# A one-core decode kernel: both MLP weights go to the head of the load queue, and the MLP is computed ahead of the query projection

## The chip, the core and the metric

The kernel runs on one core of a Trainium2 chip. The metric is the device time of one execution in microseconds (us). A difference of 0.2% is about the smallest that this measurement can tell from no change.

## The reference

One decode step for a batch of 4 tokens (`x` is 4 x 512). The input is normalised (`xn`), and two branches read it. Branch A is grouped-query attention: 32 query heads, 8 key/value heads, and of 4096 cached positions only the last W = 1024. Branch B normalises again, and runs a 512 to 1792 to 512 MLP. The output joins them.

```
xn = layernorm(x)
# branch A
q = xn @ wq                                  # 512 x 4096
k, v = last 1024 rows of the caches          # 8 kv heads, 128 wide, bf16
s = softmax(q k^T / sqrt(128)) v @ wo        # 4096 x 512
# branch B
h = gelu(layernorm(xn) @ w1 + b1)            # 512 x 1792
g = silu(h @ w2 + b2)                        # 1792 x 512
out = x + s * g
```

All data is bf16. What has to be loaded is 8 MiB of keys (8 heads x 1 MiB for the four batch entries), 8 MiB of values, 4 MiB of `wq`, 4 MiB of `wo`, and 1.75 MiB each of `w1` and `w2`: 27.5 MiB in all.

## The kernel before

**The order of work** is written out by hand. `add(engine, fn, deps)` appends one step to the program of one engine (`pe` TensorE, `dve` VectorE, `act` ScalarE, `gp` GpSimd), and `pg.dma("sp", ...)` appends a load to the program of SyncE (SP). Each engine runs its own list strictly in the order in which the steps were appended. A step first waits for its dependencies by semaphores, so a wait holds up everything behind it on that engine.

**The load queue** is SP's list: `load_k(0)`, `load_k(1)` (lines 206 to 217), `wq` in two halves of 2 MiB (219), `load_k(2)` to `load_k(7)`, then `load_v(0)`, `w1` (441), `load_v(1)`, `w2` (444), `load_v(2)` to `load_v(7)`, and `wo` in six pieces (449 to 455), the last of 128 KiB. The values of head g go into the buffer of the keys of head g, so `load_v(g)` waits for `t_last[g]`, the last transpose of that head's keys (212 to 214). The `wo` pieces wait for nothing but their place in the list.

**Front.** VectorE and ScalarE make both layernorms (247 to 264). TensorE meanwhile starts on the keys. A head's 32 key blocks are cut into 4 units of 8, so there are 32 units. `T(n)` (273) transposes the 8 blocks of unit n into PSUM and VectorE copies them out (285). There are three PSUM buffers `psK`, so `T(n)` waits for the copy of `T(n-3)`. `T(0)` to `T(7)` come first (339 to 341), then `f_xy` (343) transposes the two normalised inputs, giving `xT` for the query and `yT` for the MLP.

**Query.** `f_q` (357) multiplies `xT` with `wq`: 16 matmuls on the first half of `wq`, 16 on the second. The result is copied by VectorE and ScalarE (368, 369), transposed by `f_qT` (371), and copied into `qT` (379 to 382), which every score needs.

**Loop.** Lines 435 to 439 alternate `T(n)` and `S(n-8)`; `S` (288) computes the scores of one unit (8 matmuls with 16 columns), and after 4 units ScalarE takes the exponential of the head (306). The last 8 `S` follow without a `T` between them; the text calls these the S tail.

**Values.** `PV(g)` (310) does 32 matmuls with the values of head g, and one matmul with ones, `den` (322), that sums the denominators over the partitions. `epilogue(g)` (326) on VectorE reduces, inverts and scales (329, 332, 334). `PV(g)` waits for the exponential, for the load of V(g), and for `epilogue(g-2)`, whose PSUM it overwrites.

**MLP.** Four parts (386 to 433). `mlp1`: 14 groups of 4 matmuls with `w1` and one with the bias, then Square on ScalarE, two VectorE steps, Exp on ScalarE. `mlp2`: three VectorE steps that give `hT`. `mlp3`: 4 groups of 14 matmuls with `w2` and one with the bias, then Exp. `mlp4`: three VectorE steps that give `g`. TensorE does `mlp1` right behind `PV(0)`, and `mlp3` right behind `PV(1)` (495 to 505).

**Tail.** `to_rows` (457) regroups the attention output with 16 small matmuls, `wo` (478) does 128 matmuls in six batches, each waiting for its piece of `wo`, then come the product with `g` (512), a transpose (516), the residual (518) and the store (520).

Of the kernel before, what the change touches and what calls it, by code (L numbers as in the profile page):

```python
# [16 lines left out]
class _Program:  # L17
# [10 lines left out]
    def add(self, eng, fn, *deps):  # L28
        op = _Op(eng, fn, deps)
        self.ops[eng].append(op)  # L30
        return op
# [42 lines left out]
def bass_recurrent_scan__sliding_block_cached__mixer_channel_mlp__decode_kernel(  # L74
# [15 lines left out]
    AF = mybir.ActivationFunctionType  # L90
# [5 lines left out]
    HQ, HKV, DH = 32, 8, 128  # L96
# [4 lines left out]
    FC = F // 128  # L101
# [19 lines left out]
    wq_sb = sb([128, 4, HQ * DH], BF16)  # L121
    wo_sb = sb([128, HKV, 4, D], BF16)
    w1_sb = sb([128, 4, F], BF16)
    w2_sb = sb([128, FC, D], BF16)
# [21 lines left out]
    ident = sb([128, 128], BF16)  # L146
# [6 lines left out]
    xT = sb([128, 4, 32], BF16)  # L153
    yT = sb([128, 16], BF16)
    q_sb = sb([128, 2, 512], BF16)
    qT = sb([128, 128], BF16)
# [24 lines left out]
    psK = [nc.alloc_psum_tensor("psK%d" % i, [128, 1024], BF16) for i in range(NB)]  # L181
    psS = [nc.alloc_psum_tensor("psS%d" % i, [128, 512], F32) for i in range(2)]
    psO = [nc.alloc_psum_tensor("psO%d" % i, [128, 512], F32) for i in range(2)]
# [3 lines left out]
    pg = _Program(nc)  # L187
    add = pg.add
# [8 lines left out]
    def cache_rows(cache, g):  # L197

        return bass.AP(cache.tensor, g * SK * DH + WS * DH,
                       [[NC * DH, KR], [HKV * SK * DH, B], [1, NC * DH]])  # L200
# [5 lines left out]
    def load_k(g):  # L206
        d_k[g] = pg.dma("sp", "k%d" % g, lambda e: e.dma_start(  # L207
            kv_buf[:, g, :, :].rearrange("p c d -> p (c d)"), cache_rows(A_k_cache, g)),
            )

    def load_v(g):
        d_v[g] = pg.dma("sp", "v%d" % g, lambda e: e.dma_start(
            kv_buf[:, (HKV + g) % NS, :, :].rearrange("p c d -> p (c d)"), cache_rows(A_v_cache, g)),
            t_last[(HKV + g) % NS] if HKV + g >= NS else None)

    load_k(0)
    load_k(1)
    wq_r = A_wq.rearrange("(p c) n -> p c n", c=4)
    d_wq = [pg.dma("sp", "wq%d" % c, lambda e, c=c: e.dma_start(
        wq_sb[:, 2 * c:2 * c + 2, :], wq_r[:, 2 * c:2 * c + 2, :])) for c in range(2)]  # L220
# [52 lines left out]
    def T(n):  # L273
        g, u = n // NU, n % NU

        def fn(pe):
            last = None
            for j in range(UT):
                last = pe.transpose(psK[n % NB][:, j * 128:(j + 1) * 128],  # L279
                                    kv_buf[:, g, u * UT + j, :], ident[:, :])  # L280
            return last
        t = add("pe", fn, d_k[g], c_id, cp.get(n - NB), v_xyT if n >= LAG else None)
        if u == NU - 1:
            t_last[g] = t
        cp[n] = add("dve", lambda e: e.tensor_copy(kt_buf[:, n % NKT, :], psK[n % NB][:, 0:1024]),  # L285
                    t, sc.get(n - NKT))
# [52 lines left out]
    v_xyT = None  # L339
# [3 lines left out]
    def f_xy(pe):  # L343
# [8 lines left out]
    v_xT = add("dve", lambda e: e.tensor_copy(  # L352
        xT[:, :, 0:4], psK[1][:, 0:16].rearrange("p (c b) -> p c b", c=4)), t_xy, c_xT)
    v_xyT = add("dve", lambda e: e.tensor_copy(yT[:, :], psK[1][:, 16:32]), t_xy)


    def f_q(pe, half):
        last = None
        for c in (2 * half, 2 * half + 1):
            for m in range(HKV):  # L360
                s = m % 4
                last = pe.matmul(psO[m // 4][32 * s:32 * s + 32, 0:512], xT[:, c, :],  # L362
                                 wq_sb[:, c, m * 512:(m + 1) * 512],
                                 start=(c == 0), stop=(c == 3), tile_position=(0, 32 * s))
        return last
    add("pe", lambda pe: f_q(pe, 0), v_xT, d_wq[0])
    t_q = add("pe", lambda pe: f_q(pe, 1), d_wq[1])
    v_qr = [add("dve", lambda e: e.tensor_copy(q_sb[:, 0, :], psO[0][:, 0:512]), t_q),  # L368
            add("act", lambda e: e.activation(q_sb[:, 1, :], psO[1][:, 0:512], AF.Copy), t_q)]  # L369

    def f_qT(pe):
        last = None
        for k in range(8):
            last = pe.transpose(psK[1][:, k * 128:(k + 1) * 128],  # L374
                                q_sb[:, k // 4, (k % 4) * 128:(k % 4 + 1) * 128], ident[:, :])
        return last
    t_qT = add("pe", f_qT, v_xyT, *v_qr)

    for k in range(2):
        v_q = add("dve", lambda e, k=k: e.tensor_copy(  # L380
            bass.AP(qT, k * 64, [[128, 128], [16, 4], [4, 4], [1, 4]]),
            bass.AP(psK[1], k * 512, [[1024, 128], [32, 4], [1, 4], [128, 4]])), t_qT)

    mlp = {}

    def mlp1():
        def fn(pe):
            last = None
            for k in range(FC):
                o = psM[:, PS_H + k * 4:PS_H + (k + 1) * 4]  # L390
                for c in range(4):
                    pe.matmul(o, bass.AP(w1_sb, c * F + k, [[4 * F, 128], [FC, 128]]),  # L392
                              yT[:, c * 4:(c + 1) * 4], start=(c == 0), stop=False)
                last = pe.matmul(o, bass.AP(b1_sb, k, [[F, 1], [FC, 128]]), ones_bf[0:1, 0:4],  # L394
                                 start=False, stop=True)
            return last
        h = psM[:, PS_H:PS_H + FC * 4]
        t = add("pe", fn, v_xyT, d_w1, d_b1)
        a = add("act", lambda e: e.activation(u2_sb[:, :], h, AF.Square), t)  # L399
        v = add("dve", lambda e: e.tensor_scalar(t_sb[:, :], u2_sb[:, :], GELU_K, 1.0,  # L400
                                                 op0=ALU.mult, op1=ALU.add), a)
        v = add("dve", lambda e: e.tensor_tensor(t2_sb[:, :], t_sb[:, :], h, ALU.mult), v)
        mlp["e"] = add("act", lambda e: e.activation(ge_sb[:, :], t2_sb[:, :], AF.Exp,
                                                     scale=-GELU_A), v)

    def mlp2():
        h = psM[:, PS_H:PS_H + FC * 4]
        v = add("dve", lambda e: e.tensor_single_scalar(e1_sb[:, :], ge_sb[:, :], 1.0, ALU.add),
                mlp["e"])
        v = add("dve", lambda e: e.reciprocal(r_sb[:, :], e1_sb[:, :]), v)  # L410
        mlp["h"] = add("dve", lambda e: e.tensor_tensor(hT[:, :], h, r_sb[:, :], ALU.mult), v)  # L411

    def mlp3():
        def fn(pe):
            last = None
            for c in range(4):
                o = psM[:, PS_Z + c * 4:PS_Z + (c + 1) * 4]
                for k in range(FC):
                    pe.matmul(o, w2_sb[:, k, c * 128:(c + 1) * 128], hT[:, k * 4:(k + 1) * 4],  # L419
                              start=(k == 0), stop=False)  # L420
                last = pe.matmul(o, b2_sb[0:1, c * 128:(c + 1) * 128], ones_bf[0:1, 0:4],
                                 start=False, stop=True)
            return last
        t = add("pe", fn, mlp["h"], d_w2, d_b2)
        mlp["ez"] = add("act", lambda e: e.activation(
            ez_sb[:, :], psM[:, PS_Z:PS_Z + 16], AF.Exp, scale=-1.0), t)

    def mlp4():
        v = add("dve", lambda e: e.tensor_single_scalar(d1_sb[:, :], ez_sb[:, :], 1.0, ALU.add),
                mlp["ez"])  # L430
        v = add("dve", lambda e: e.reciprocal(rz_sb[:, :], d1_sb[:, :]), v)
        mlp["g"] = add("dve", lambda e: e.tensor_tensor(
            g_sb[:, :], psM[:, PS_Z:PS_Z + 16], rz_sb[:, :], ALU.mult), v)

    NUN = HKV * NU
    for n in range(LAG, NUN + LAG):
        if n < NUN:
            T(n)
        S(n - LAG)
    load_v(0)  # L440
    d_w1 = pg.dma("sp", "w1", lambda e: e.dma_start(
        w1_sb[:, :, :], B_w1.rearrange("(p c) f -> p c f", c=4)))
    load_v(1)
    d_w2 = pg.dma("sp", "w2", lambda e: e.dma_start(
        w2_sb[:, :, :], B_w2.rearrange("(p c) o -> p c o", c=FC)))
    for g in range(2, HKV):
        load_v(g)

    wo_r = A_wo.rearrange("(g p i) o -> p g i o", g=HKV, i=4)
# [44 lines left out]

    for g in range(HKV):
        PV(g)
        if g == 0:
            mlp1()
        if g >= 1:
            epilogue(g - 1)  # L500
        if g == 1:
            mlp2()
            mlp3()
        if g == 2:
            mlp4()
    epilogue(HKV - 1)
    rows = to_rows(0, HKV)
    for k in range(len(d_wo)):
# [65 lines left out]
```

## Time and profile before

| what | value |
|---|---|
| median of 4 runs | 77.29 us (77.23 to 77.46) |
| the profiled execution itself | 77.27 us |
| its span, first to last instruction | 75.4 us |
| around the span (77.27 less 75.4) | 1.9 us |
| mean granted TensorE clock | 0.744 of full speed |
| TensorE busy | 52.5 us (70%) |
| VectorE busy | 38.1 us (51%) |
| ScalarE, GpSimd busy | 9.0 and 4.5 us |
| loaded on SP's queue | 28.84 MB |
| mean rate over the span | 385 GB/s |

Every other time in this document that is taken from the profile is in microseconds from the start of this span. TensorE has two rows in the profile: PE is the matmuls, PEld the loads of their weights, which run beside them. The page also cuts the span into 40 slices of 1.9 us and gives the busy share of each in tenths. For a load, the trace gives the moment at which SP issued it and the time from there to its landing; an issue can be tens of microseconds ahead of the landing, since the queue holds many loads.

### The profile page before, as it was taken

Reading aid. Unit: us, or ns where it says so; the run is one execution under the profiler, and the core shown is the slowest. Engines: PE = TensorE matmul, PEld = TensorE weight load, DVE = VectorE, ACT = ScalarE, POOL = GpSimd, SP = SyncE. Lnnn points to the kernel's source line nnn. Section 1 sums busy time; section 2 is a strip of 40 time slices with the busy share of each in tenths; the row PEclk is TensorE's granted clock in tenths of the full one; section 3 lists DMA queues with packets and bytes.
Section 4 is the critical chain, followed back from the end, with each engine's and each line's share of the span. In section 5 each row is a group of like instructions: output and inputs, shape, how many; then the busy total and the mean of one; then the engine's idle time right before and its main releaser. Section 6 shows DMA issues by size and latency. Waiting matters only on the chain.

```text
span 75.4 us, 2396 instructions
## 1 busy us (share of the span) xinstructions
PE 52.5 (70%) x1095; PEld 46.5 (62%) x1107; DVE 38.1 (51%) x84; ACT 9.0 (12%) x16; POOL 4.5 (6%) x13
## 2 busy tenths in 40 slices
PE   0008993500558999999999972999729897845970
PEld 0008982200218999999999862999729865815950
DVE  0778997100033589999998400000592587782010
ACT  0611000000054030330330630000200000000000
POOL 6970000000000000000000000000000000000000
PEclk9999999985555599999999999555555555555555
DMA  0899999999999999999999998999999999999700
GB/s 2 276 405 404 449 444 443 426 435 378 417 452 417 417 422 439 430 400 473 404 417 456 403 458 379 426 417 426 435 417 439 404 413 417 417 406 421 274 20 2
DMA packets 4213, 28.99 MB, mean 385 GB/s; under 512 B 486, under 2 KB 619, under 8 KB 1644
## 3 DMA queue, kind: packets, MB, share of 16 engines
q1 hardware_dynamic: 4160, 28.84, 91.7%
q8 instruction: 8, 0.13, 0.6%
q10 hardware_dynamic: 44, 0.01, 0.1%
q14 instruction: 1, 0.01, 0.0%
HBM read 28.85 MB, written 0.00 MB: 383 GB/s over the span
## 4 chain that ended last, share of the span: by engine, by line
PE 57%; DMA 22%; DVE 10%; issue 5%; SPq 2%; ACT 0%
DMA wq_sb<-in_A_wq_dram 22%; PE psK L279 16%; PE psS L298 10%; PE psM L392 6%; PE psO L316 6%; PE psM L486 5%; DVE den_sb L329 4%; PE psM L394 3%; PE psO L362 3%; PE psM L419 3%; PE psS L322 2%; SPq L207 2%; DVE rden L332 1%; PE psK L374 1%; DVE OTb L334 1%
## 5 line engine op out<-in xcount | busy, mean ns | idle before, releaser
L279 PE MATMUL psK<-ident,kv_buf 128*128 128x128 bf16 x256 | 21.5, 239 | 5.9 <-DMA kv_buf<-in_A_k_cache_dram 5.9
L285 DVE COPY kt_buf<-psK 128x1024 bf16<-128x1024 bf16 x32 | 20.9, 689 | 2.7 <-PE psK L279 2.6
L279 PEld LDWEIGHTS psK<-ident,kv_buf 128*128 128x128 bf16 x256 | 17.3, 108 | 6.2 <-DMA kv_buf<-in_A_k_cache_dram 5.9
L298 PE MATMUL psS<-qT,kt_buf 128*128 128x16 bf16 x256 | 10.4, 170 | 0.6 <-issue 0.2
L298 PEld LDWEIGHTS psS<-qT,kt_buf 128*128 128x128 bf16 x256 | 9.6, 97 | 1.1 <-issue 0.3
L316 PEld LDWEIGHTS psO<-P_buf,kv_buf 128*128 128x128 bf16 x256 | 7.5, 103 | 2.1 <-issue 2.1
L316 PE MATMUL psO<-P_buf,kv_buf 128*128 128x16 bf16 x256 | 8.0, 174 | 1.0 <-DVE OTb L334 0.6
L392 PE MATMUL psM<-yT,w_sb 128*128 128x4 bf16 x56 | 5.7, 204 | 1.9 <-issue 1.8
L362 PE MATMUL psO<-wq_sb,xT 128*32 128x512 bf16 x32 | 2.9, 504 | 5.5 <-DMA wq_sb<-in_A_wq_dram 5.1
L306 ACT ACTIVATE P_buf<-psS 128x512 bf16<-128x512 f32 x8 | 4.8, 597 | 16.1 <-PE psS L298 16.1
L329 DVE TENSOR_REDUCE den_sb<-psS 128x16 f32<-128x512 f32 x8 | 5.5, 690 | 1.4 <-PE psO L316 1.2
L400 DVE TENSOR_SCALAR t_sb<-u_sb 128x56 f32<-128x56 f32 x1 | 0.2, 193 | 11.4 <-ACT u_sb L399 11.4
L392 PEld LDWEIGHTS psM<-yT,w_sb 128*128 128x128 bf16 x56 | 4.5, 153 | 2.3 <-issue 2.1
L362 PEld LDWEIGHTS psO<-wq_sb,xT 128*32 128x32 bf16 x32 | 0.8, 112 | 6.7 <-DMA wq_sb<-in_A_wq_dram 5.6
L368 DVE CAST q_sb<-psO 128x512 bf16<-128x512 f32 x1 | 0.7, 692 | 8.2 <-PE psO L362 8.2
L486 PE MATMUL psM<-OW,wo_sb 128*128 128x4 bf16 x128 | 3.7, 166 | 0.5 <-DVE OW L472 0.5
L486 PEld LDWEIGHTS psM<-OW,wo_sb 128*128 128x128 bf16 x128 | 3.6, 104 | 0.6 <-issue 0.6
L419 PE MATMUL psM<-hT,w_sb 128*128 128x4 bf16 x56 | 2.1, 167 | 1.8 <-DVE hT L411 1.8
L394 PE MATMUL psM<-ones_bf,b_sb 1*128 1x4 bf16 x14 | 3.0, 215 | 0.0
L419 PEld LDWEIGHTS psM<-hT,w_sb 128*128 128x128 bf16 x56 | 1.8, 105 | 1.9 <-DVE hT L411 1.9
L369 ACT ACTIVATE q_sb<-psO 128x512 bf16<-128x512 f32 x1 | 0.6, 597 | 14.7 <-PE psO L362 14.7
L332 DVE RECIPROCAL rden<-den_sb 128x16 f32<-128x16 f32 x8 | 2.0, 253 | 0.3
(63 smaller groups left out, 28.3 us busy)
## 6 DMA issues: line engine op xcount, KB each, us to landing
kv_buf<-in_A_k_cache_dram SPq DMA_DIRECT2D x8, 1024.0 KB, 21.4
kv_buf<-in_A_v_cache_dram SPq DMA_DIRECT2D x8, 1024.0 KB, 22.2
wq_sb<-in_A_wq_dram SPq DMA_DIRECT2D x2, 2048.0 KB, 14.0
w_sb<-in_B_w_dram SPq DMA_DIRECT2D x2, 1792.0 KB, 30.9
wo_sb<-in_A_wo_dram SPq DMA_DIRECT2D x3, 1024.0 KB, 24.6
wo_sb<-in_A_wo_dram SPq DMA_DIRECT2D x1, 512.0 KB, 21.4
wo_sb<-in_A_wo_dram SPq DMA_DIRECT2D x1, 384.0 KB, 18.1
wo_sb<-in_A_wo_dram SPq DMA_DIRECT2D x1, 128.0 KB, 17.9
```

What stands on the lines that cost most here:

```text
L279: last = pe.transpose(psK[n % NB][:, j * 128:(j + 1) * 128], kv_buf[:, g, u * UT + j, :], ident[:, :])
L285: cp[n] = add("dve", lambda e: e.tensor_copy(kt_buf[:, n % NKT, :], psK[n % NB][:, 0:1024]), t, sc.get(n - NKT))
L298: last = pe.matmul(psS[g % 2][:, c * 16:(c + 1) * 16], kt_buf[:, n % NKT, j * 128:(j + 1) * 128], qT[:, g * 16:(g + 1) * 16], start=False, ...
L306: ex[g] = add("act", lambda e: e.activation(P_buf[:, g, :], psS[g % 2][:, 0:512], AF.Exp, scale=SCALE), sc[n])
L316: last = pe.matmul(pso[:, 0:16], kv_buf[:, (HKV + g) % NS, c, :], P_buf[:, g, c * 16:(c + 1) * 16], start=(c == 0), stop=(c == NC - 1))
L329: v = add("dve", lambda e: e.tensor_reduce(den_sb[:, cs], bass.AP(psS[g % 2], 0, [[512, 128], [1, 16], [16, NC]]), AX.X, ALU.add), den[g])
L332: v = add("dve", lambda e: e.reciprocal(rden[:, cs], den_sb[:, cs]), v)
L362: last = pe.matmul(psO[m // 4][32 * s:32 * s + 32, 0:512], xT[:, c, :], wq_sb[:, c, m * 512:(m + 1) * 512], start=(c == 0), stop=(c == 3), ...
L392: pe.matmul(o, bass.AP(w1_sb, c * F + k, [[4 * F, 128], [FC, 128]]), yT[:, c * 4:(c + 1) * 4], start=(c == 0), stop=False)
L394: last = pe.matmul(o, bass.AP(b1_sb, k, [[F, 1], [FC, 128]]), ones_bf[0:1, 0:4], start=False, stop=True)
L419: pe.matmul(o, w2_sb[:, k, c * 128:(c + 1) * 128], hT[:, k * 4:(k + 1) * 4], start=(k == 0), stop=False)
L486: last = pe.matmul(psM[:, PS_W + c * 4:PS_W + (c + 1) * 4], wo_sb[:, g, i, c * 128:(c + 1) * 128], OW[:, i, g * 4:(g + 1) * 4], start=firs ...
```

## The change

On SP's list `w1` becomes the first load, ahead of the keys of head 0, and `w2` comes behind the keys of head 1, ahead of both halves of `wq`. The values are then loaded in one plain row. The four parts of the MLP are unchanged in themselves. Their calls move from between the `PV` steps to a place directly behind `f_xy`, ahead of `f_q`, on TensorE, VectorE and ScalarE alike.

```diff
+    d_w1 = pg.dma("sp", "w1", lambda e: e.dma_start(
+        w1_sb[:, :, :], B_w1.rearrange("(p c) f -> p c f", c=4)))
     load_k(0)
     load_k(1)
+    d_w2 = pg.dma("sp", "w2", lambda e: e.dma_start(
+        w2_sb[:, :, :], B_w2.rearrange("(p c) o -> p c o", c=FC)))
     wq_r = A_wq.rearrange("(p c) n -> p c n", c=4)
     d_wq = [pg.dma("sp", "wq%d" % c, lambda e, c=c: e.dma_start(
         wq_sb[:, 2 * c:2 * c + 2, :], wq_r[:, 2 * c:2 * c + 2, :])) for c in range(2)]
...
     v_xyT = add("dve", lambda e: e.tensor_copy(yT[:, :], psK[1][:, 16:32]), t_xy)
+    mlp = {}
...
+    mlp1()
+    mlp2()
+    mlp3()
+    mlp4()
...
-    load_v(0)
-    d_w1 = pg.dma("sp", "w1", lambda e: e.dma_start(
-        w1_sb[:, :, :], B_w1.rearrange("(p c) f -> p c f", c=4)))
-    load_v(1)
-    d_w2 = pg.dma("sp", "w2", lambda e: e.dma_start(
-        w2_sb[:, :, :], B_w2.rearrange("(p c) o -> p c o", c=FC)))
-    for g in range(2, HKV):
+    for g in range(HKV):
         load_v(g)
...
     for g in range(HKV):
         PV(g)
-        if g == 0:
-            mlp1()
         if g >= 1:
             epilogue(g - 1)
-        if g == 1:
-            mlp2()
-            mlp3()
-        if g == 2:
-            mlp4()
```

More of the change, by code (lines that the diff above doesn't have):

```diff
@@ L354, in bass_recurrent_scan__sliding_block_cached__mixer_channel_mlp__decode_kernel @@
     v_xyT = add("dve", lambda e: e.tensor_copy(yT[:, :], psK[1][:, 16:32]), t_xy)
[L357 to L382, printed above, removed]
     mlp = {}
@@ L433, in mlp4, with f_q, f_qT @@
             g_sb[:, :], psM[:, PS_Z:PS_Z + 16], rz_sb[:, :], ALU.mult), v)
+    mlp1()
+    mlp2()
+    mlp3()
+    mlp4()
+    def f_q(pe, half):
+        last = None
+        for c in (2 * half, 2 * half + 1):
+            for m in range(HKV):
+                s = m % 4
+                last = pe.matmul(psO[m // 4][32 * s:32 * s + 32, 0:512], xT[:, c, :],
+                                 wq_sb[:, c, m * 512:(m + 1) * 512],
+                                 start=(c == 0), stop=(c == 3), tile_position=(0, 32 * s))
+        return last
+    add("pe", lambda pe: f_q(pe, 0), v_xT, d_wq[0])
+    t_q = add("pe", lambda pe: f_q(pe, 1), d_wq[1])
+    v_qr = [add("dve", lambda e: e.tensor_copy(q_sb[:, 0, :], psO[0][:, 0:512]), t_q),
+            add("act", lambda e: e.activation(q_sb[:, 1, :], psO[1][:, 0:512], AF.Copy), t_q)]
+    def f_qT(pe):
+        last = None
+        for k in range(8):
+            last = pe.transpose(psK[1][:, k * 128:(k + 1) * 128],
+                                q_sb[:, k // 4, (k % 4) * 128:(k % 4 + 1) * 128], ident[:, :])
+        return last
+    t_qT = add("pe", f_qT, v_xyT, *v_qr)
+    for k in range(2):
+        v_q = add("dve", lambda e, k=k: e.tensor_copy(
+            bass.AP(qT, k * 64, [[128, 128], [16, 4], [4, 4], [1, 4]]),
+            bass.AP(psK[1], k * 512, [[1024, 128], [32, 4], [1, 4], [128, 4]])), t_qT)
     NUN = HKV * NU
```

## The prediction

> **What bounds the kernel now.** I read the 40 slices first, to see which resource is never idle.
>
> ```profile
> PE   0008993500558999999999972999729897845970
> PEclk9999999985555599999999999555555555555555
> DMA  0899999999999999999999998999999999999700
> ```
>
> The transfer engines are full from the second slice to the 37th, about 2 to 70 us. The change moves loads but adds and removes no byte, so the end of the stream should stay where it is. I then read when single loads land (issue plus time to landing).
>
> ```profile
> L219 SPq DMA_DIRECT2D wq_sb<-in_A_wq_dram x2: 563/590/616, 2.1 to 2.8; - x2
> ...
> DMA to landing us min/median/max: 11.2/14.0/16.8
> ```
> ```profile
> L454 SPq DMA_DIRECT2D wo_sb<-in_A_wo_dram x2: 435/2942/5449, 53.9 to 54.4; - x2
> ...
> DMA to landing us min/median/max: 17.9/18.0/18.1
> ```
>
> The halves of `wq` land at 2.1 + 11.2 = 13.3 and 2.8 + 16.8 = 19.6, the last piece of `wo` at 54.4 + 17.9 = 72.3. By the same view K0 lands at 5.9, K1 at 8.5, K2 at 22.0, K7 at 34.2, V7 at 62.3. From K2 to V7 lie 16.5 MiB and 40.3 us: 2.44 us per MiB. Last I read TensorE's timeline.
>
> ```profile
> 13.44 1.05 PE L362 MATMUL psO<-wq_sb,xT 128*32 128x512 bf16 x16 [0.32 <-DVE yT L354]
> 19.63 1.90 PE L362 MATMUL psO<-wq_sb,xT 128*32 128x512 bf16 x16 [5.14 <-DMA wq_sb<-in_A_wq_dram]
> ```
> ```profile
> 43.56 0.95 PE L316 MATMUL psO<-P_buf,kv_buf 128*128 128x16 bf16 x32
> ...
> 44.58 0.17 PE L392 MATMUL psM<-yT,w_sb 128*128 128x4 bf16 x1
> 46.57 0.26 PEld L392 LDWEIGHTS psM<-yT,w_sb 128*128 128x128 bf16 x3 [2.07 <-issue]
> 46.58 0.34 PE L392 MATMUL psM<-yT,w_sb 128*128 128x4 bf16 x3 [1.83 <-issue]
> ...
> 56.08 0.53 PE L419 MATMUL psM<-hT,w_sb 128*128 128x4 bf16 x14 [1.81 <-DVE hT L411]
> ...
> 68.91 3.71 PE L486 MATMUL psM<-OW,wo_sb 128*128 128x4 bf16 x128 [0.51 <-DVE OW L472]
> 72.66 0.18 DVE L512 TENSOR_TENSOR sg_sb<-psM,g_sb 128x16 f32<-128x16 f32 x1 [3.89 <-PE psM L486]
> ```
>
> TensorE waits for `wq` until 19.63 and from then on hardly at all. The 128 `wo` matmuls run without a hole from 68.91 to 72.63, 29 ns each. The last four need the piece that landed at 72.3, and come at 72.5. So two chains end together here: the stream at 72.3, and TensorE's work at 72.63. From the last matmul the span has 2.75 us left, which the change doesn't touch. **Whatever TensorE saves is worth nothing below a floor of about 72.6; whatever it loses counts in full.**
>
> **What the change takes from the late stage.** From PV(0) at 43.56 to the first `wo` matmul at 68.91 are 25.35 us. Without the MLP the stage is eight `PV` groups in a row. PV(4) starts at 61.25, so four groups with the regrouping behind them take 68.91 - 61.25 = 7.66 us. Two groups (62.53 to 65.36) take 2.83, or 1.415 each. Eight groups: 7.66 + 4 x 1.415 = 13.3 us. The MLP and its waits therefore cost 25.35 - 13.3 = **12.05 us**, 1.83 of it the hole at 44.75.
>
> **What it puts in front.** `w1` (1.75 MiB, 4.3 us) is now ahead of K0 and K1, and 3.5 MiB (8.6 us) ahead of the second half of `wq`. K0 lands at 5.9 + 4.3 = 10.2, K1 at 12.8, `w2` near 17, `wq` at 19.6 + 8.6 = 28.2. The cover for the MLP is thus mostly bought by the change itself. TensorE's steps in its new order:
>
> - T(0) to T(7): in the window from 5.9 to 10.3, 48 of these transposes take 4.4 us, 0.73 per unit. From 10.2 the eighth ends near 16.0, with K1 in time for T(4). Its copy (0.65) and `f_xy` with the copies behind it (0.78, from 12.66 to 13.44) give `yT` at 17.4. If the clock rises earlier, VectorE's 0.65 per unit from K1 on sets it: 16.4. I take 17.25.
> - `mlp1`: 14 groups at 0.482 (46.58 to 53.33 holds them) make 6.75. A group takes as long at clock 1.0 (ahead of 47) as at 0.5. Ends at 24.0.
> - Square, Exp and `mlp2`: Square 0.24, Exp 0.25, three VectorE steps with gaps 0.98 (55.06 to 56.04). ScalarE still holds the square-root table; the load for Exp, 1.28 at 22.20 in the row of line 306, now falls between Square and Exp and hides only 0.45 of VectorE work. Chain 2.75, against 2.0 with the load hidden. TensorE stands idle: its next step in line is `mlp3`. 26.75.
> - `mlp3`: 2.4 (56.08 to 58.47). 29.15. `w2` is long there. `mlp4` is off TensorE's path.
> - `f_q`: all 32 matmuls now come behind the wait; before, 16 of them hid in it. At clock 0.5 sixteen took 1.93 (19.63 to 21.56), at 1.0 1.05. The MLP's narrow matmuls ran from 47 on at 0.5, busy as PE was, so I take 3.86, with 2.1 as the lower end. **Ends at 33.0, against 21.56: 11.45 us later.** `wq`, at 28.2, is not what is waited for.
>
> From `f_q` to PV(0) I leave the 22.0 us of before (21.56 to 43.56): K2 to K7 land from 30.6 to 42.8, ahead of their use. The clock came up at 26.4 there, 4.9 us behind `f_q`. A unit takes 1.05 us at 0.5 and 0.65 at 1.0, and a step of the clock lasted 3.4 us or multiples, so this is worth up to 0.6 less or 1.2 more. The bounds of the delay are 8.1 (16.4, a hidden table load, `f_q` at full clock) and 12.65.
>
> **The hole at 44.75** names no releaser. Both MLP weights had landed (40.9, 47.7 for the one used later). But one of eight transfers of another kind starts at 44.2:
>
> ```profile
> q8 instruction: 8, 0.13, 0.6%
> ```
>
> Between the starts of the fetches from 32.0 to 70.5 the PE and PEld rows count 1530 instructions in six stretches, 255 each. The hole follows the fastest stretch, S tail and PV(0), some 65 instructions per us, and I read it as a fetch that came late. The change takes 70 + 60 matmuls with as many weight loads, 260 instructions, from behind this place to ahead of it: all but the same distance as between fetches. So a boundary falls at the same place again, 4 instructions on. The stall may be nothing (seven of the eight fetches show none as long) or 1.83; being at the same place but hanging on a queue, it gets two thirds, **1.2 us**. The Trainium skill, "Runtime: NRT & Kernel Launch", section "Instruction fetch mechanics", says that instructions come in 16 KiB blocks of 256, and that crossing a block is mostly hidden. The 1.83 us speak against the second half; by it the stall would be zero and the result that of the first rival. Another page, "ScalarE: Activation LUTs", section "What ACT_TABLE_LOAD costs", adds a drain of 1.38 us to the 1.28 of a table load, which would speak further against the change; the trace shows 1.28 and a ScalarE that is free again, and by the page the MLP chain would be 1.4 us longer.
>
> **The sum.** First `wo` matmul: 68.91 - 12.05 + 11.45 + 1.2 = 69.51, last 73.23, against 72.63: **0.6 us later**. The profiled execution took 77.27, so 77.9; the median is 77.29, so nothing changes by it.
>
> **What costs nothing.** V2's load waits on SP for T(11), near 39 instead of 27.4. The queue holds everything up to V1, which lands at 47.7, so 8 us of cover. V7 goes out near 53 and V6 lands at 59.9: 6 us. The `wo` pieces behind it go out from 53.5 to 57, and land from 64.8. V7 itself lands at 62.3, and PV(7) would come at 65 or later. `b1` and `b2` come on ScalarE's queue at the start, as before.
>
> **Rivals.**
>
> 1. *The floor holds (15%).* If the delay and the stall together stay under 12.05, TensorE reaches the last `wo` piece before it lands, and the landing at 72.3 with four matmuls behind it ends near 72.6. For: the sum misses that by 0.6 and the stall can be zero. Against: PEld and PE show a hole at just this place. Time 77.25 (77.15 to 77.4).
> 2. *The stream ends earlier (15%), the side opposite to my forecast.* One place decides: the second half of `wq` took 6.3 us behind the first (4.8 behind K1 for as many bytes), and all later loads kept these 1.4 us. If the new order doesn't lose them, the last piece lands at 70.9, and with no stall the `wo` matmuls end at 68.91 - 12.05 + 11.45 + 3.72 = 72.03: 76.7. It needs the delay and stall together under 11.9; with a delay of 8.1, 75.9. Against: whatever held one engine there may do so in any order.
> 3. *The stream starves (5%).* If the loop slips more than 6 to 8 us further, loads of V come too late onto an empty queue and each us of it is added to the end: 79 and over. Against: the 6 to 8 us.
> 4. *The MLP doesn't fit in the wait:* by my sum it ends 0.95 behind the landing of `wq`. This is part of the forecast, not beside it.
>
> **Numbers.** Forecast as summed, TensorE ends last: 65%, 77.5 to 79.2. With rivals 1 and 2 at 15% each and 3 at 5%: slower by over 0.2% 70%, within 0.2% 15%, faster 15% (0.2% is about what a measurement of this kernel can tell from no change). The highest bound, delay 12.65 and stall 1.83, gives 77.9 + 1.2 + 0.63 = 79.7; the range leaves out this corner and the far end of rival 2: 76.7 to 79.2.
>
> **What would show it.** In the new profile: `mlp1` from about 17 to 24; `f_q` from 29 to 33 at clock 0.5, with 32 matmuls in a row; PV(0) near 55; a hole of up to 1.83 without releaser near PV(0)'s end; `wo` matmuls from 69.5 without a hole; the last landing at 72.3 as before. I am wrong if the last `wo` matmuls wait for their load, if `f_q` runs at full clock, or if SP is seen waiting while the transfer row drops below 9.

## The result, and the profile after

The changed kernel is slower by 0.65%: ratio to the kernel before 1.0065, 95% interval 1.0045 to 1.0085. With the 77.36 of the kernel before in the same sets of runs this is about 77.9 us. Its profiled execution took 77.84 with a span of 75.9, against 77.27 and 75.4. Of its 38 runs 23 lie more than 1.5% above the fastest and are left out of the ratio, so that the median of all 38, 79.34 (77.57 to 81.18), stands higher than the ratio says, for a cause that no run here looked for.

The slices of the page after, 1.9 us each:

```profile
PE   0000039947999049977999999999909878754970
PEclk9999999999855555559999999999997555555555
DMA  1899999999999999999999999999999999999400
```

The transfers stay full until the 37th slice here too, so the later loads of values starved nothing. The lowered clock (the fives) now covers the MLP from 20.2 on and ends with `f_q`. The nines ahead of 13.4 are no full clock: the trace has no record of the clock before that, and the transposes follow each other every 107 ns there, against 56 ns behind it. The PE row keeps a 0 at 55 us, where the hole was foretold.

TensorE's timeline after, with two lines of ScalarE's (start, length, operation, and in brackets the idle time ahead of it and what ended that):

```profile
17.99 0.40 PE L369 MATMUL psM<-yT,w_sb 128*128 128x4 bf16 x4 [0.34 <-DVE yT L359]
...
25.05 1.28 ACT L380 ACT_TABLE_LOAD   x1
26.34 0.25 ACT L380 ACTIVATE ge_sb<-t_sb 128x56 f32<-128x56 f32 x1
...
27.67 0.53 PE L396 MATMUL psM<-hT,w_sb 128*128 128x4 bf16 x14 [2.89 <-DVE hT L388]
...
29.98 3.60 PE L423 MATMUL psO<-wq_sb,xT 128*32 128x512 bf16 x32
...
54.01 0.95 PE L321 MATMUL psO<-P_buf,kv_buf 128*128 128x16 bf16 x32
56.93 0.95 PE L321 MATMUL psO<-P_buf,kv_buf 128*128 128x16 bf16 x32 [1.97 <-issue]
62.60 0.31 PE L321 MATMUL psO<-P_buf,kv_buf 128*128 128x16 bf16 x6 [0.44 <-issue]
69.57 3.58 PE L490 MATMUL psM<-OW,wo_sb 128*128 128x4 bf16 x128 [0.51 <-DVE OW L476]
```

The MLP runs from 17.99 to 30.05 in TensorE's list, `f_q` follows it without a wait, and behind `PV(0)` stands a hole of 1.97 that ends by no releaser, and a smaller one of 0.44 later. The 128 `wo` matmuls run without a hole, as before, but 0.66 later (69.57 against 68.91). The stream ends later as well. The load of the last piece of `wo`, after (the two pieces of that line go out at 55.7 and 56.2):

```profile
L458 SPq DMA_DIRECT2D wo_sb<-in_A_wo_dram x1: 4165/4165/4165, 56.2 to 56.2; - x1
...
DMA to landing us min/median/max: 16.6/16.6/16.6
```

56.2 + 16.6 = **72.8, against 72.3 before**, for the same bytes. So both of the chains that ended together before, the stream and TensorE's work, end together again, each half a microsecond later. Whether one of them alone makes the loss, and why the stream moved at all, is what the experiments ask.

### The profile page after: what moved, and what is told of

It is laid out like the page before. It is cut to its first block, busy times and chain, and to the rows that moved or that the text cites. A ratio compares the mean times of both kernels' runs of the same rounds, so it can differ in the third digit from the quotient of the medians.

```text
span 75.9 us, 2397 instructions
## 1 busy us (share of the span) xinstructions
PE 51.7 (68%) x1096; PEld 44.7 (59%) x1107; DVE 38.6 (51%) x84; ACT 9.0 (12%) x16; POOL 4.5 (6%) x13
## 4 chain that ended last, share of the span: by engine, by line
PE 56%; DVE 16%; DMA 12%; another core or an unknown queue 6%; issue 4%; ACT 2%; SPq 1%
PE psK L284 18%; DMA kv_buf<-in_A_k_cache_dram 12%; PE psS L303 7%; PE psM L369 6%; DVE kt_buf L290 6%; PE psO L321 6%; PE psM L490 5%; PE psO L423 5%; DVE den_sb L334 4%; PE psM L371 3%; PE psM L396 3%; PE psS L327 2%; ACT L380 2%; DVE rden L337 1%
## 5 line engine op out<-in xcount | busy, mean ns | idle before, releaser
L284 PE MATMUL psK<-ident,kv_buf 128*128 128x128 bf16 x256 | 20.0, 228 | 10.7 <-DMA kv_buf<-in_A_k_cache_dram 10.7
L284 PEld LDWEIGHTS psK<-ident,kv_buf 128*128 128x128 bf16 x256 | 15.8, 102 | 11.2 <-DMA kv_buf<-in_A_k_cache_dram 10.7
L303 PE MATMUL psS<-qT,kt_buf 128*128 128x16 bf16 x256 | 10.2, 169 | 0.6 <-DVE qT L441 0.2
L423 PE MATMUL psO<-wq_sb,xT 128*32 128x512 bf16 x32 | 3.6, 631 | 0.0
L327 PE MATMUL psS<-P_buf,ones_bf 128*128 128x512 bf16 x4 | 2.3, 586 | 0.0
(63 smaller groups left out, 27.8 us busy)
## 6 DMA issues: line engine op xcount, KB each, us to landing
wo_sb<-in_A_wo_dram SPq DMA_DIRECT2D x1, 512.0 KB, 17.4
wo_sb<-in_A_wo_dram SPq DMA_DIRECT2D x1, 128.0 KB, 16.6
```

The lines of the kernel that those rows point to most:

```text
L284: last = pe.transpose(psK[n % NB][:, j * 128:(j + 1) * 128], kv_buf[:, g, u * UT + j, :], ident[:, :])
L303: last = pe.matmul(psS[g % 2][:, c * 16:(c + 1) * 16], kt_buf[:, n % NKT, j * 128:(j + 1) * 128], qT[:, g * 16:(g + 1) * 16], start=False, ...
L327: den[g] = add("pe", lambda pe: pe.matmul(psS[g % 2][:, 0:512], ones_bf[:, :], P_buf[:, g, :], start=True, stop=True), ex[HKV - 2 + g % 2] ...
```

## The experiments

Theories are named as in the expectations on record: A says that TensorE's later chain makes the loss, B that the stream, which ends later, makes it. The kernels stand beside each other here; "last `wo`" is the end of the last `wo` matmul, times are those of each profiled execution, ratios are to the kernel before on the same chip.

| kernel | profiled | ratio, 95% interval | last landing | last `wo` |
|---|---|---|---|---|
| before | 77.27 | 1 | 72.3 | 72.62 |
| after | 77.84 | 1.0065 [1.0045, 1.0085] | 72.8 | 73.15 |
| a_no_mlp | 77.76 | 1.0052 [1.0022, 1.0082] | 72.9 | 73.27 |
| b_no_mlp | 77.10 | 0.9971 [0.9945, 0.9997] | 72.3 | 72.61 |
| a_pad64 | 78.65 | 1.0124 [1.0068, 1.0180] | 73.1 | 74.17 |
| b_pad64 | 77.29 | 0.9983 [0.9960, 1.0006] | 72.4 | 72.71 |
| b_open_w1 | 77.76 | 1.0058 [1.0034, 1.0081] | 73.0 | 73.27 |
| a_open_k0 | 77.26 | 0.9976 [0.9957, 0.9994] | 72.3 | 72.63 |
| open_halves | 77.02 | 0.9967 [0.9936, 0.9999] | 72.2 | 72.48 |
| k0_full | 77.39 | 0.9991 [0.9956, 1.0027] | 72.2 | 72.74 |
| k01_first | 77.10 | 0.9994 [0.9973, 1.0015] | 72.2 | 72.52 |
| a_fq_gap | 78.18 | 1.0107 [1.0065, 1.0150] | 72.9 | 73.51 |
| order_only | 84.17 | 1.0927 [1.0861, 1.0992] | 73.1 | 79.49 |

### The MLP's work taken out of both kernels: a_no_mlp and b_no_mlp

Both keep all loads of their parent but leave out the computation of the MLP (`g` is set to 1, so the output is x + s). TensorE is then far ahead, and the end is the stream's alone.

```diff
-    mlp1()
-    mlp2()
-    mlp3()
-    mlp4()
+    mlp["g"] = add("dve", lambda e: e.memset(g_sb[:, :], 1.0), d_b1, d_b2)
```

a_no_mlp, from the kernel after:

> The changed kernel with the MLP's computation left out: g is filled with ones, so the output is x + s; all loads stay, in the new order. TensorE then has 12 us less in front of the query. Theory A (TensorE's chain alone made the change 0.5 us slower; the stream's floor is where it was): f_q ends near 30, right behind wq, the wo matmuls reach their last piece before it lands, it lands at 72.3 as before, and the time is about 77.2, level with before. Theory B (the new order itself ends the stream later, 72.8 in the changed kernel against 72.3): the last piece lands at 72.8 again, the last wo matmul ends near 73.1, and the time is 77.7 to 77.9, that of the changed kernel.

b_no_mlp, from the kernel before:

> The kernel before with the MLP's computation left out: g is filled with ones, so the output is x + s; all loads stay, in the old order. This shows the floor of the old order. Both theories: 12 us of TensorE work go from the late stage, the last piece of wo lands near 72.3 as before, and all but the last four wo matmuls are done by then; the time is 77.0 to 77.3, no more than 0.3 us below before. If the floor reading is wrong and TensorE's chain alone sets the end, the time falls by several us.

TensorE's timeline in a_no_mlp:

```profile
72.68 0.59 PE L487 MATMUL psM<-OW,wo_sb 128*128 128x4 bf16 x16 [0.53 <-DMA wo_sb<-in_A_wo_dram]
```

and in b_no_mlp:

```profile
72.01 0.60 PE L486 MATMUL psM<-OW,wo_sb 128*128 128x4 bf16 x16 [0.31 <-DMA wo_sb<-in_A_wo_dram]
```

In both the last matmuls wait for their load (`<-DMA`). Theory B's marks for a_no_mlp came true (72.8 and 77.7 to 77.9 expected, 72.9 and 77.76 measured), and the floor expected of b_no_mlp did too. With 12 us of work gone from TensorE the new order of loads still takes 1.0052 of the time before, and the old order 0.9971. Two things follow. The kernel before stands within 0.2 us of its floor (77.10 against 77.27 in the profiled executions), so nothing that only frees TensorE could have gained more. And **the new order of loads alone suffices for the whole loss**: the stream moved by 0.6 us with the same bytes. That is theory B.

### The hole behind PV(0): a_pad64 and b_pad64

To see whether the hole is a late instruction fetch, 64 narrow matmuls whose result is never read go ahead of `T(0)`, 128 instructions with their weight loads, half of the distance between two fetches.

```diff
+    def f_pad(pe):
+        last = None
+        for k in range(64):
+            last = pe.matmul(psM[:, 256:260], ident[:, :], ones_bf[:, 0:4], start=True, stop=True)
+        return last
+    add("pe", f_pad, c_id)
```

a_pad64, in the kernel after:

> The changed kernel with 64 narrow matmuls (4 columns, about 30 ns each, never read) ahead of the first transpose, while TensorE waits for the first keys: 128 instructions more, half of the distance between two instruction fetches, so the boundary that fell at the end of PV(0) moves 128 instructions ahead, into the loop. If the hole of 2 us is a late instruction fetch, it goes or shrinks below 1 us, and the wo matmuls start near 67.6 instead of 69.57. Theory A: the time falls to about 77.3, the floor of before. Theory B: it falls by less than 0.2 us, since the stream ends at 72.8. If the hole belongs to PV(0) itself, it stays at 2 us.

b_pad64, in the kernel before:

> The kernel before with the same 64 narrow matmuls in front. If the hole of 1.83 us at 44.75 is a late instruction fetch, it moves or shrinks, and the wo matmuls start near 67.1 instead of 68.91. Both theories have the time unchanged within 0.2 us, since the last piece of wo lands at 72.3 whatever TensorE does. A gain of over 1 us would say that TensorE's chain sets the end of the kernel before.

TensorE's timeline in a_pad64:

```profile
54.26 0.94 PE L303 MATMUL psS<-qT,kt_buf 128*128 128x16 bf16 x32 [0.27 <-issue]
55.06 1.98 PE L321 MATMUL psO<-P_buf,kv_buf 128*128 128x16 bf16 x64
...
57.64 0.94 PE L321 MATMUL psO<-P_buf,kv_buf 128*128 128x16 bf16 x30 [0.37 <-DVE OTb L339]
60.38 0.22 PE L321 MATMUL psO<-P_buf,kv_buf 128*128 128x16 bf16 x2 [1.80 <-issue]
```

The hole left its place behind `PV(0)` (55.06 in this kernel, with no hole behind it) and came up again 126 instructions further on, behind the 30th matmul of `PV(2)`, with 1.80. A fetch starts 0.4 us ahead of it, at 58.18. The pads move the old place 128 instructions ahead, into the S tail, where a hole of 0.27 is left (54.0); the next place then falls about as far behind `PV(0)`, and the long hole is there. The count of instructions shows the same in every trace. In the rows of PE and PEld, all holes of over 0.3 us that end by no releaser stand behind 943, 1196 or 1197, 1449 or 1453, 1704 or 1708, and 1958 instructions in the 13 kernels of the table, some 250 to 256 apart, whatever work is done there. The long one stands behind 1196 before, 1453 after and 1708 here; the 0.27 here stands behind 1454. The hole hangs on the number of instructions ahead of it and not on any data, as a fetch does. Why it is long at some of these places and short or absent at others stays open. The expected gain failed, because the hole did not vanish but came up at the next place, and because the pads delay TensorE's start: the clock first comes up at 16.7 instead of 13.4, PV(0) starts 1.05 later, and `wo` at 70.61. In b_pad64 the hole at 44.75 is gone (0.25 is left at 42.45, behind 1199 instructions), the matmuls of `mlp1` run on at 44.45 and 44.73, and the end is this:

```profile
72.12 0.59 PE L493 MATMUL psM<-OW,wo_sb 128*128 128x4 bf16 x16 [0.34 <-DMA wo_sb<-in_A_wo_dram]
```

TensorE gained its 1.8 us and waits for the load at the end instead. The time is the same, 0.9983 [0.9960, 1.0006]: the floor once more.

### Which load opens the stream: b_open_w1 and a_open_k0

The trace's records of single packets tell when each of the 16 transfer engines finishes its part of a load. Before, K0 opens the stream, and its 16 parts land between 5.4 and 5.9. After, `w1` opens it, in pieces of 14 KB to a row where those of K0 have 8 KB, and its parts land between 6.9 and 8.2, the last three of them 1.3 behind the first. Theory B1: this skew is carried to the end. The two kernels exchange just this between the no-MLP pair (both leave out the MLP as above, `g` = 1).

```diff
 # b_open_w1, from b_no_mlp
+    d_w1 = pg.dma("sp", "w1", lambda e: e.dma_start(
+        w1_sb[:, :, :], B_w1.rearrange("(p c) f -> p c f", c=4)))
     load_k(0)
...
     load_v(0)
-    d_w1 = pg.dma("sp", "w1", lambda e: e.dma_start(
-        w1_sb[:, :, :], B_w1.rearrange("(p c) f -> p c f", c=4)))
     load_v(1)
 # a_open_k0, from a_no_mlp
+    load_k(0)
     d_w1 = pg.dma("sp", "w1", lambda e: e.dma_start(
         w1_sb[:, :, :], B_w1.rearrange("(p c) f -> p c f", c=4)))
-    load_k(0)
     load_k(1)
```

> The kernel before, again without the MLP's computation (g filled with ones, output x + s), and with one change in the load order: w1 opens the queue, w2 stays behind V1. Nothing else moves; TensorE has some 8 us to spare. In the changed kernel the 16 parts of the opening load w1 land up to 1.3 us apart (6.9 to 8.2), in the kernel before those of K0 0.5 us (5.4 to 5.9), and a later instruction fetch that falls on a part that is already behind adds up. Theory B1 (the opening load makes the skew, and the skew ends the stream later): the parts of w1 land over 1 us apart, the last piece of wo lands at 72.7 to 73.1 instead of 72.3, and the time is 77.6 to 77.9, against 77.16 with K0 opening. Theory B2 (the late end comes from the rest of the new order, wq behind both weights, or from where the fetches fall): it lands at 72.3 and the time stays at 77.1 to 77.3.

> The changed kernel without the MLP's computation (g filled with ones, output x + s), with one change in the load order: K0 opens the queue, w1 comes second, the rest as in the changed kernel. Theory B1: the parts of K0 land within 0.6 us of each other, the last piece of wo lands at 72.3 to 72.5, and the time falls from 77.85 to 77.1 to 77.3. Theory B2: the last piece lands at 72.8 or later and the time stays at 77.7 to 78.0.

What the transfers moved from 69 to 74 us, GB/s in 40 slices of 0.125 us, before, after, in b_open_w1 and in a_open_k0:

```profile
GB/s 287 410 475 459 360 295 483 443 418 401 221 361 270 254 221 197 188 197 139 172 172 131 107 57 0 0 0 0 0 0 0 0 0 0 0 0 0 0 0 0
```
```profile
GB/s 467 344 377 459 410 418 352 352 320 328 287 270 328 279 221 213 213 123 172 164 115 98 74 49 49 25 49 49 8 0 0 0 0 0 0 0 0 0 0 0
```
```profile
GB/s 434 442 377 369 418 426 385 361 442 360 246 262 238 205 221 213 197 156 131 123 123 82 41 25 25 25 16 25 25 0 0 0 0 0 0 0 0 0 0 0
```
```profile
GB/s 361 459 361 443 418 377 410 426 385 385 303 254 197 180 164 172 172 172 147 147 123 139 139 66 0 0 0 0 0 0 0 0 0 0 0 0 0 0 0 0
```

If all 16 engines ended together, each row would fall from 400 to 0 at once. All four fall in a slope of some two microseconds instead, in which one engine after the other runs out of work; the first is through at 70.2 to 70.6 in every kernel. Where `w1` opens (second and third row) the slope has a tail of 25 to 49 up to 72.6, one or two engines that still work alone. Where K0 opens (first and fourth) it is over at 72.0. To the old order the opening by `w1` alone adds what the change added (1.0058 against 0.9971), and to the new order the opening by K0 alone takes it away (0.9976 against 1.0052). The intervals of the two pairs do not touch. **B1 holds: the load that opens the stream decides.** In a_open_k0 the parts of K0 land 0.4 apart, and the last piece of `wo` at 72.3 again. The other traces say the same. In the six kernels that K0 opens, its parts land 0.2 to 0.5 apart and those of the last piece of `wo` 1.6 to 1.8; in the six that the whole `w1` opens, 1.2 to 1.6 and 2.6 to 2.8.

### The opening load in two halves: open_halves and w1_halves

If the long pieces make the skew, `w1` at the head as two loads with 7 KB to a row should not. open_halves does this to a_no_mlp (no MLP, `g` = 1), w1_halves to the full kernel after.

```diff
-    d_w1 = pg.dma("sp", "w1", lambda e: e.dma_start(
-        w1_sb[:, :, :], B_w1.rearrange("(p c) f -> p c f", c=4)))
+    d_w1 = [pg.dma("sp", "w1%d" % i, lambda e, i=i: e.dma_start(
+        w1_sb[:, 2 * i:2 * i + 2, :],
+        B_w1.rearrange("(p c) f -> p c f", c=4)[:, 2 * i:2 * i + 2, :])) for i in range(2)]
```

> The changed kernel without the MLP's computation (g filled with ones, output x + s), with w1 still at the head of the queue but loaded as two loads, each of half of every partition's row: 7 KB in one piece per partition instead of 14 KB. K0's pieces are 8 KB and opened evenly. Theory C1 (it is the long pieces that open unevenly): the parts of the first half land within 0.6 us of each other, the last piece of wo at 72.3 to 72.5, time 77.1 to 77.3 against 77.85 with the whole load. Theory C2 (it is w1's place in the tensor, or its being another tensor than the keys, and not the length of the pieces): the parts land over 1 us apart, time 77.7 to 78.0.

> The changed kernel, all work done, with w1 loaded in the same two halves at the head of the queue. TensorE's work and the moments at which K0 and K1 come are those of the changed kernel within 0.5 us, so this tells TensorE's chain from the stream. If C1 holds: theory A (TensorE's chain by itself is 0.5 us late) gives the last wo matmul near 72.7 to 73.2 with no wait for the load, and 77.5 to 77.8; theory B (the stream alone did it) gives wo matmuls that wait for their load and 77.1 to 77.3. If C2 holds, 77.8 by both.

open_halves gives 0.9967 [0.9936, 0.9999], and its last landing is 72.2: so `w1` can open the stream at no loss if it comes in two halves. The evenness that C1 expected (0.6) is only partly there, though: the parts of the first half land 4.7 to 5.6, 0.9 apart, against 0.5 for K0 and 1.3 for the whole `w1`. In the profiled execution a part of the result is that no fetch met the two engines that lagged by 0.9; the first fetch met the next one, at 0.6, and put it 2.2 behind. That the length of the pieces is the cause is not shown: the halves also make the first load half as large, and their pieces of 7 KB land less evenly than K0's of 8 KB. w1_halves gives 1.0013 [0.9959, 1.0068], an interval that holds both answers; its profiled execution was an outlier of 201.91 us, in which `f_q` alone took 10.5 us, so its trace shows nothing of the others. The run leaves open whether TensorE's chain alone would cost as much as the stream.

### The full kernel with K0 at the head: k0_full

All work of the kernel after; only the first two loads change places (the second part of the diff of b_open_w1 and a_open_k0, here on the kernel after).

> The changed kernel, all work done, with K0 opening the queue and w1 second. K1, which holds T(4) to T(7) up, lands at 12.6, half a us ahead of the changed kernel; MLP and query come as much earlier, near f_q's end at 33.2. The stream ends at 72.3 as measured without the MLP. Theory A: the last wo matmul comes at 72.6 to 72.9, and at 74 if the clock rises a step later: time 77.3 to 77.5, or 78.5. Theory B: 77.1 to 77.3, with wo matmuls that wait for their load.

```profile
56.52 0.98 PE L321 MATMUL psO<-P_buf,kv_buf 128*128 128x16 bf16 x32 [1.97 <-issue]
...
69.19 3.55 PE L490 MATMUL psM<-OW,wo_sb 128*128 128x4 bf16 x128 [0.51 <-DVE OW L476]
```

This timeline has the same hole of 1.97 and the same unbroken `wo`, each 0.4 earlier than after, since K0 comes first and `f_q` ends at 33.24 instead of 33.62. The last landing is 72.2. The ratio is 0.9991 [0.9956, 1.0027]: the loss is gone with two loads exchanged. One exchange moves both chains, so this run does not part them. Its marks were those of theory A (72.6 to 72.9 and 77.3 to 77.5 expected, 72.74 and 77.39 measured, no `wo` matmul waits), so with K0 in front it is TensorE's chain that ends last, by a little. It shows that the early MLP need not cost anything: with K0 ahead of `w1` it neither loses nor gains.

### The MLP weights behind K0 and K1: k01_first

```diff
-    d_w1 = pg.dma("sp", "w1", lambda e: e.dma_start(
-        w1_sb[:, :, :], B_w1.rearrange("(p c) f -> p c f", c=4)))
     load_k(0)
     load_k(1)
+    d_w1 = pg.dma("sp", "w1", lambda e: e.dma_start(
+        w1_sb[:, :, :], B_w1.rearrange("(p c) f -> p c f", c=4)))
     d_w2 = pg.dma("sp", "w2", lambda e: e.dma_start(
```

> The changed kernel, all work done, with w1 behind the keys of heads 0 and 1 instead of in front of them: K0, K1, w1, w2, wq, then as before. T(0) to T(7) run from 5.9 as in the kernel before, mlp1 from 13.4 to 20.2, mlp3 ends near 25.3, the first query matmuls run while the second half of wq lands at 28, and f_q ends near 29.8 instead of 33.6. Theory A with B1: TensorE's chain ends 2 to 3 us earlier and the stream at 72.3: time 77.1 to 77.4, level with the kernel before. B2: the stream ends at 72.8 or later, time 77.6 to 77.9.

```profile
71.92 0.60 PE L490 MATMUL psM<-OW,wo_sb 128*128 128x4 bf16 x16 [0.32 <-DMA wo_sb<-in_A_wo_dram]
```

`f_q` ends at 29.89 here, 3.7 earlier than after, and `wo` starts at 67.21, 1.7 earlier than before. TensorE thus really gains from an early MLP, in this order, and the timeline shows where the gain goes: into waits for the pieces of `wo`. The ratio is 0.9994 [0.9973, 1.0015].

### f_q's first half into MLP's waiting time: a_fq_gap

```diff
+    mlp1()
     add("pe", lambda pe: f_q(pe, 0), v_xT, d_wq[0])
+    mlp2()
+    mlp3()
+    mlp4()
     t_q = add("pe", lambda pe: f_q(pe, 1), d_wq[1])
```

> The changed kernel, all work done, with the first 16 query matmuls moved ahead of mlp2, into the 2.9 us in which TensorE waits for the MLP's exponential; the first half of wq lands at 22.3, ahead of that. Theory A: f_q ends 1.6 to 1.9 us earlier, and so does TensorE's chain, if the clock still rises at the start of the loop; without the long dense stretch it may rise one 3.4 us step later, which gives back up to 1.3. Theory B: whatever TensorE gains, the last piece of wo lands at 72.8 and the time stays at 77.7 to 77.9; the wo matmuls are seen waiting for their loads.

This gained nothing: 1.0107, against 1.0065 for the kernel after, with intervals that overlap. No `wo` matmul waits for its load, so theory B's mark is missing here, and its time was passed (78.18). The first half fills the hole in which TensorE waits for `hT` (24.86 to 26.76), and `f_q` ends at 32.04, 1.58 earlier than after. But PV(0) starts at 54.23, later than after. What took its place shows in a table of one stretch (length, busy time of PE, then the clock, the transfers' share and GB/s at the end of the line):

```profile
34.00:36.00 2.00, 1.78 (x23) 0.50 1.03 434
```

The clock stays at 0.50 until near 37.8, 5.7 behind the end of an `f_q` in two parts of 16 matmuls. In the kernel after, with 32 in a row, it came up at once, as the same table shows (its windows are `f_q` and the loop behind it; here with the busy times of all engines, and clock, share and GB/s again last):

```profile
29.98:33.62 3.64, 3.61 (x33) 1.08 (x32) 0.60 (x3) 0.18 (x1) 0.00 (x0) 0.50 1.02 428
33.90:48.00 14.10, 13.17 (x301) 12.85 (x307) 12.26 (x21) 2.73 (x5) 0.00 (x0) 1.00 1.01 424
```

The gain of 1.58 went into slower steps of the loop: PV(0) starts 0.22 later than after, where the expectation allowed for 1.3 given back. Whether the split `f_q` held the clock down is not shown. In a_no_mlp, whose two parts of 16 ended at 29.83, the clock rose at 33.8, the same moment as after:

```profile
31.00:33.70 2.70, 2.48 (x30) 0.50 1.01 425
33.90:36.00 2.10, 2.05 (x51) 1.00 1.02 433
```

### The order of loads without the early MLP: order_only

The loads as after, the MLP's steps where they were before.

```diff
+    d_w1 = pg.dma("sp", "w1", lambda e: e.dma_start(
+        w1_sb[:, :, :], B_w1.rearrange("(p c) f -> p c f", c=4)))
     load_k(0)
     load_k(1)
+    d_w2 = pg.dma("sp", "w2", lambda e: e.dma_start(
+        w2_sb[:, :, :], B_w2.rearrange("(p c) o -> p c o", c=FC)))
...
-    d_w1 = pg.dma("sp", "w1", lambda e: e.dma_start(
-        w1_sb[:, :, :], B_w1.rearrange("(p c) f -> p c f", c=4)))
     load_v(1)
-    d_w2 = pg.dma("sp", "w2", lambda e: e.dma_start(
-        w2_sb[:, :, :], B_w2.rearrange("(p c) o -> p c o", c=FC)))
```

> The load order of the changed kernel with the MLP computed where the kernel before computes it, between the PV steps. This prices the two halves of the change. By the prediction's sum the second half of wq lands near 28, f_q ends at 29.6 to 29.9 instead of 21.56 (its first half again hides in the wait), 8.1 to 8.3 us later, and the 12.05 us of MLP stay in the late stage: last wo matmul near 80.8, time 85.2 to 85.8. If the late stage has slack that the sum doesn't see, the time is 81 or less.

```profile
27.50 1.90 PE L366 MATMUL psO<-wq_sb,xT 128*32 128x512 bf16 x16 [2.84 <-DMA wq_sb<-in_A_wq_dram]
```

The second half of `wq` is waited for until 27.50, `f_q` ends at 29.40, 7.84 later than before (the landing of `wq`, 19.63 then, moved by 7.87). `wo` starts at 75.94, 7.03 later: nearly all of the delay is passed on, since TensorE has little slack behind `f_q`. The time, 84.17 to 85.14 in four runs, stays somewhat under the 85.2 to 85.8 expected. The early MLP then wins back 84.17 - 77.84 = 6.3 us of what its loads cost. It is not the 12.05 that leave the late stage, because `f_q` comes at 33.62 instead of 29.40.

## Why the prediction was right, and where it was not

**The time and the sign were right, TensorE's sum to 0.06 us** (first `wo` matmul at 69.57, foretold 69.51), and the sum was made of three errors that cancel. That it fits so closely is luck:

| step | foretold | measured after |
|---|---|---|
| K0, K1, `w2`, `wq` land | 10.2, 12.8, 17, 28.2 | 10.7, 13.1, 17.4, 27.8 |
| `yT` | 17.25 | 17.9 |
| `mlp1` | 6.75 | 6.8 (17.99 to 24.77) |
| end of `mlp1` to `mlp3` | 2.75 | 2.90 |
| `mlp3` | 2.4 | 2.4 |
| `f_q`, clock | 3.86 at 0.5 | 3.64 at 0.5 |
| end of `f_q` | 33.0 | 33.62 |
| `f_q` to PV(0) | 22.0 | 20.39 |
| PV(0) to `wo` without holes | 13.3 | 13.15 |
| holes | 1.2 | 1.97 + 0.44 |
| last landing | 72.3 | 72.8 |

- *The delay of `f_q`* was 12.06 (33.62 - 21.56), 0.6 more than summed. Nearly all of it is `yT`, 0.65 late: K0 landed 0.5 later than by its bytes, which is the uneven opening again. The parts of the MLP chain fit to 0.15, and they fitted because their durations were those of the same instructions at their later place. The table load stood exposed as foretold, 25.05 to 26.33. Of the 1.38 us drain that "ScalarE: Activation LUTs", section "What ACT_TABLE_LOAD costs" in the Trainium skill, adds to it, this trace shows nothing: Exp starts 0.01 behind the load, and the load 0.01 behind Square.
- *The loop* was 1.6 shorter than the 22.0 taken over. The prediction gave this at most 0.6. What failed there is that the clock would rise some 4.9 us behind `f_q`, as it had: it came up 0.3 behind (33.9). In the three kernels with 32 matmuls in a row it rose close to their end, from 0.5 ahead of it to 0.3 behind (a_pad64, k0_full, after); in those with two parts of 16, with a gap between them, 3.7 to 6.8 later (k01_first, order_only, a_fq_gap, b_open_w1, open_halves and a_open_k0, from their granted clocks). That the row of 32 is the cause was not tried by itself, and the moments speak for another reading as much: the clock rose at 33.5 to 34.6 in a_no_mlp, order_only, k01_first and open_halves too, where `f_q` had ended by 29.9, so in the kernel after `f_q` may just have ended when the clock was about to rise.
- *The hole* is a fetch of instructions, by the pads and by the counts of all traces, and came at the place and nearly the size of before (1.97, by 1.83). Two thirds of it was a mean between nothing and all, and all was right; the 0.44 is the next place in the count (1704) and was not in the sum. The working behind it was less firm than it looked: the rows from 32.0 to 70.5 count 1501 instructions, not 1530, and from one start of a fetch to the next 88 to 342, so the 255 was a mean. The holes, some 250 to 256 apart, bear it out. The fetch begins at 54.4, as the fetch of before began at 44.2, and TensorE stands still at 54.96. "Runtime: NRT & Kernel Launch", section "Instruction fetch mechanics", calls the crossing mostly hidden; here 1.97, 1.80 and 1.83 stood open in three kernels.
- *V2's and V7's loads*: V2 went out at 37.83, V7 at 52.0, V5 landed at 58.1 and V7 at 63.0. Nothing starved. Rival 3 was rightly small.

**The step that failed is the floor: "The change moves loads but adds and removes no byte, so the end of the stream should stay where it is."** It moved from 72.3 to 72.8, and with no MLP on TensorE to 72.9. In a_no_mlp, where TensorE reaches `wo` at 66.88 and then waits for the loads of this order, the ratio is 1.0052 [1.0022, 1.0082]. Hence rival 1 (TensorE in time, 77.25) was out of reach in this order but for a rare execution (of the 12 of a_no_mlp, eleven took 77.69 to 78.01 and one 77.19), and rival 2 (the stream ends earlier) had the wrong sign: what it took for a loss of `wq`'s place is, by the packets of the trace, an instruction fetch that meets one of the 16 engines at 17.1, in whatever load is then under way. In b_pad64 the first fetch starts at 12.8, and there it is the first half of `wq` whose last part comes late (14.8 instead of 13.3). The prediction named TensorE alone as what ends last. In the profiled execution that is so, by a little: `wo` runs without a hole. But take that chain away and the time stays. For the old order the floor was right: in b_no_mlp the last `wo` matmul ends at 72.61, by the foretold 72.6. So the forecast named one of two chains that each end at the measured time, and missed the other.

What stays open: whether TensorE's chain alone would cost the full 0.65% (w1_halves was to tell and did not); why `w1` as the opening load leaves three engines behind; which engine a fetch meets; and what moves the clock.

No version here beats the kernel before by more than its own distance to the floor: b_no_mlp, a_open_k0 and open_halves, all without the MLP's work, stand at 0.9967 to 0.9976.

## What to carry to other kernels

Where a saturated load stream ends last, its end is that of its slowest engine and not of its bytes: look at when the parts of the last and of the first load land, and open the stream with a load whose parts land together (here K0, not the whole `w1`). Before moving work off an engine, take that work out and look at the time that is left: here 12 us of work were worth 0.2. And what is put ahead of a load that another step waits for costs that step nearly its transfer time: 3.5 MiB, 8.5 us at 2.44 us per MiB, put `f_q` 7.84 us later in order_only.

## What the runs showed of the hardware

- **The opening of the stream can be uneven, and the unevenness stays.** Parts of the first load land 1.2 to 1.6 apart with `w1` in 14 KB pieces, 0.9 with its half in 7 KB pieces, 0.2 to 0.5 with K0 in 8 KB pieces. Once the stream runs, the pieces of 16 and 8 KB go at 38.2 to 38.6 ns per KB on each engine, the 4 KB pieces of `wo` at 39.8.
- **An instruction fetch costs the stream too.** One fetch is a packet of 16 KB on one of the 16 engines that takes 0.88 to 0.97 us while the stream runs, and the part of the load on that engine comes 1.3 to 1.6 late from then on: before, the fetch at 17.1 does this to the second half of `wq` (17.7 to 19.6). A fetch that meets an engine that already lags adds to it. After, the one at 54.4 does: V4 lands from 52.9 to 54.6, V5 from 55.3 to 58.1, so the spread goes from 1.8 to 2.8, and the last piece of `wo` lands from 70.2 to 72.8 (before, 70.5 to 72.3).
- **A fetch can stall TensorE.** The longest hole of this kind is 1.4 to 2.1 us in twelve of the 13 kernels of the table, and one can place it by counting instructions (0.25 in b_pad64). Most fetches leave no hole of over 0.3 us.
- **A busy TensorE row does not hold the clock up.** From 47 to 68 us before, with PE busy for 16.98 of these 21 us, most of it with matmuls of 4 and 16 columns, it stayed at 0.50. In the traces of the 13 kernels the clock keeps one value for 3.4 us or a multiple of it (3.4, 6.8, 10.2, 13.7, 17.1, 20.5, 23.9), so its changes come in steps of 3.4 us.
